# Handing some bf16-bit shifts of an attention kernel from VectorE to GpSimd

## The chip, the cores and the metric

The kernel runs on one core of a Trainium2 chip. The metric is the device time of one execution, in microseconds. Before the change it is 1596.61 us, the median of three runs (1596.51 to 1596.66).

## The reference

The reference is a stack of four residual layers on x of 2048 tokens by 512 channels: attention, MLP, attention, MLP, all in bf16, each after a layer norm. Both attentions use the same weights, and so do both MLPs.

```python
def _A_ref(x, wqkv, wo):            # 32 heads of 16 channels
    q, k, v = ...                   # from x @ wqkv
    scores = jnp.einsum("bhqd,bhkd->bhqk", q, k) * Dh ** -0.5
    p = _softmax(scores, axis=-1)
    o = jnp.einsum("bhqk,bhkd->bhqd", p, v)
    return o.transpose(0, 2, 1, 3).reshape(B, S, D) @ wo

def _B_ref(x, w1, b1, w2, b2):
    h = _gelu(jnp.einsum("bsd,df->bsf", _layernorm(x), w1) + b1)
    return jnp.einsum("bsf,fd->bsd", h, w2) + b2

x = x + _A_ref(_layernorm(x), A_wqkv, A_wo)
x = x + _B_ref(_layernorm(x), B_w1, B_b1, B_w2, B_b2)
# and both once more
```

What matters here is the softmax: 32 heads x 2048 x 2048 exponentials in each attention.

## The kernel before

**The work.** The layers are called L = 1 and L = 3 (each with the MLP behind it). The queries are cut into units of 512 tokens, qc (in L = 3 the last unit is cut into two of 256). The heads are in eight groups of four, hg. A *segment* is one head group of one unit against all 2048 keys (the first unit of each layer is cut into two parts by keys). It consists of score tiles: one key block of 128 tokens, one head, 512 query columns; a full segment has 16 x 4 = 64 of them. For each tile PE multiplies keys and queries into a PSUM bank (L1401, four heads side by side in rows of the array), something turns scores into exponentials, and PE multiplies those with the values into bank ACCB (L1579, four heads side by side in columns). The 17th column of the values is ones, so that the softmax's denominator comes along.

**Two ways to an exponential.** ScalarE takes two or three tiles at once from PSUM and writes bf16 into PT (L1386). In five of sixteen key blocks (DK = 3, 6, 9, 12, 15) a tile may go to VectorE instead, which uses the fact that a number written as an integer into the bits of a bf16 is roughly its exponential. The *load* (`d_load`, L1478) adds BITS0 to the scores in PSUM and writes them as uint16 into a slot of `dp`; read as bf16, this is a rough exponential. To make it exact enough, three more *readings* of it are made, with 32, 64 and 96 added to the bits (SHIFT; `job_d`, L1509), each into a `dp` slot of its own, and PE sums all four with values that are scaled by WSHIFT (`vs`, L1169, made by GpSimd and kept in DRAM). Two tiles make a batch (DBATCH), so that a reading is one instruction of 1024 elements.

**What sets the order.** Nothing is written by hand. A planner on the host (`Sched`, `Prog`) simulates the engines with a cost for each operation, and the order in which it picks tasks becomes the fixed order of each engine's instructions; semaphores for the dependencies are added at the end. It picks, for each engine, the ready task of least priority number (`best`), and then the engine whose pick comes first (`run`). What it takes for true of costs is in `Prog.op` (L106): VectorE is free again 0.08 us before an operation's end (OVERLAP). An operation marked "fast" on VectorE becomes longer by the last GpSimd operation's `hit` where the two overlap (L140 to L147):

```python
if eng == "pool":
    self.hit = (op.t0, op.t0 + dur, lat or 0.0)
elif lat == "fast":
    if self.hit[0] < op.t0 + dur and op.t0 < self.hit[1]:
        dur += self.hit[2]
```

**How many tiles VectorE gets** is decided while planning. `take_d` (L1411) hands it a tile if VectorE isn't booked over 1.3 us ahead and has no more than DBACK = 2.0 us of tasks pending, if a slot of `dp` is free and fewer than DFLY = 4 batches are under way, and if a PSUM bank is free: DLANE (bank 5), or MISCB (bank 7). It is called beside every group for ScalarE (`flow_scores`), after every VectorE operation (`d_solo`), and in gaps of PE (`fill_pe`). Tiles that nobody took by the segment's end go to ScalarE. So VectorE's planned free time turns into tiles that ScalarE needn't do. `refill` then puts matmuls of zeros (L1307, L1309, L1311) into gaps of PE.

**Around the change.** `job_d` is started when a batch's loads are in the plan. For each of the three readings it gets a `dp` slot, sets a priority and submits the task. It goes on to the next when the task has been planned (not when it has ended). The priority `pr` is 0.15 if no tile of the segment is left and it is the one being summed, 0.5 if fewer than DURGE = 8 are left, and 2.5 else: behind all else that VectorE has. `try_pv` (L1526) plans the value matmuls of a reading when its planned end is at most PV_NEAR = 0.7 us away; PE's order is then fixed. GpSimd's other work is Q scaling (`job_qt`, L1144), the scaled values (L1169), layer norm (L858 to L868), and the small operations of the score bound and of the joining of the two parts (L1003 to L1007, L1622 to L1633).

Of the kernel before, what the change touches and what calls it, by code (L numbers as in the profile page):

```python
# [14 lines left out]
ALU = mybir.AluOpType  # L15
# [20 lines left out]
SHIFT = (0, 32, 64, 96)  # L36
# [231 lines left out]
def I(fn, reads=(), writes=(), dur=0.3, same_ok=(), lat=None):  # L268
    return (fn, tuple(reads), tuple(writes), tuple(same_ok), dur, lat)
# [242 lines left out]
class Builder:  # L512
# [988 lines left out]
    def job_d(self, bt):  # L1501

        S_ = self.S_
        u, n, sg = bt["unit"], len(bt["tiles"]), bt["tiles"][0][0]
        N = 512 * n
        for k in range(1, len(SHIFT)):
            v = yield ("get", "dp", sg["i"])
            pr = 0.15 if not self.left(sg) and sg is self.segs[self.acc_seg] else 0.5 if self.left(sg) < DURGE else 2.5
            yield Task("dve", pr, [I(lambda e, k=k, v=v: e.tensor_scalar(out=self.dp[:, v, 0:N], in0=self.dp[:, u, 0:N], scalar1=float(SHIFT[k]), scalar2=None, op0=ALU.add),  # L1509
                                     [("dp", u, w) for w in range(n)], [("dp", v, w) for w in range(n)] + self.dres(v), 0.150 + 0.2605e-3 * N, (), "fast")])  # L1510
            self.d_ready(bt, k, v, range(n))
        self.flying -= 1
        self.use_done(("dp", u))
# [425 lines left out]
```

## Time and profile before

| engine | part of the work | instructions | busy us | mean ns |
|---|---|---|---|---|
| PE | scores, L1401 | 4608 | 672.3 | 358 |
| PE | value matmuls of PT, L1579 | 3544 | 467.1 | 358 |
| PE | value matmuls of the load and the three readings, L1579 | 4256 | 659.7 | 357 |
| ScalarE | exponentials, L1386 | 1274 | 1449.7 | 1259 |
| VectorE | loads, L1478 | 944 | 632.6 | 681 |
| VectorE | readings, L1509 | 1434 | 557.4 | 430 |
| GpSimd | Q scaling, L1144 | 84 | 72.2 | 860 |
| GpSimd | scaled values, L1169 | 72 | 60.5 | 842 |

The profiled execution has a span of 1594.1 us, with TensorE's clock fully granted. Durations overlap: VectorE starts the next instruction before the last has ended, and four matmuls run side by side on PE, so that a group's busy time isn't instructions times mean. A busy digit is the share of a fortieth of the span (40 us) in tenths:

```profile
DVE  7689999989999899989999898999899989999793
ACT  6999999999999999989999998999999999999996
POOL 5585312001220012103212217310001000020010
```

GpSimd is busy at the start (layer norm and the bounds of the first layer) and around 1000 us, and nearly idle else. The waits of VectorE and ScalarE, longest first, are these:

```profile
DVE dp L1478 <- PE ps L1401: 58.2, 81, 3.0
DVE xres L1758 <- PE ps L1756: 15.5, 8, 4.2
...
ACT PT L1386 <- PE ps L1401: 32.2, 80, 4.4
ACT h L1810 <- PE ps L1713: 11.8, 4, 8.1
```

The numbers are the sum in us, the times, and the longest.

### The profile page before, as it was taken

The page shows a single profiled execution, that of the slowest core. Times are in us where ns is not written, and L with a number is a line of the kernel's source. Part 1 is how long each engine was busy: PE and PEld are TensorE (multiplying, and loading weights), DVE is VectorE, ACT ScalarE, POOL GpSimd, SP SyncE. Part 2 cuts the span into 40 slices and gives each one's busy share as a digit, 9 for nine tenths or more (in the row PEclk, how much of TensorE's full clock was granted, in tenths as well). Part 3 has the DMA queues.
Part 4 walks back from the last instruction along what each step waited for, and adds up shares of the span by engine and source line. Part 5 has one row for each costly group of instructions (what it writes and reads, how often), then busy time and mean ns, then how long its engine had stood idle before and what let it go on. Part 6 is the DMA issues. An engine that isn't in the chain of part 4 may idle for free.

```text
span 1594.1 us, 39159 instructions
## 1 busy us (share of the span) xinstructions
PE 1538.6 (97%) x16364; PEld 479.4 (30%) x16497; DVE 1450.3 (91%) x3202; ACT 1528.0 (96%) x1357; POOL 333.9 (21%) x574
## 2 busy tenths in 40 slices
PE   9999999999999999999999999999999999999998
PEld 3222222222222222222222223222222222344444
DVE  7689999989999899989999898999899989999793
ACT  6999999999999999989999998999999999999996
POOL 5585312001220012103212217310001000020010
PEclk9999999999999999999999999999999999999999
DMA  6662012112321223223722233211101100221100
GB/s 172 116 142 87 29 31 40 48 41 59 81 48 50 44 53 78 57 53 86 139 44 62 53 68 78 61 25 21 34 14 38 28 19 22 40 48 30 41 25 21
DMA packets 212465, 88.80 MB, mean 56 GB/s; under 512 B 183835, under 2 KB 206656, under 8 KB 212288
## 3 DMA queue, kind: packets, MB, share of 16 engines
q1 hardware_dynamic: 212288, 86.29, 24.0%
q8 instruction: 129, 2.11, 0.6%
q14 instruction: 48, 0.39, 0.1%
HBM read 34.65 MB, written 19.48 MB: 34 GB/s over the span
## 4 chain that ended last, share of the span: by engine, by line
PE 51%; DVE 28%; ACT 17%; issue 2%; POOL 0%; DMA 0%; POOLq 0%; DVEq 0%
PE ps L1401 18%; ACT PT L1386 15%; PE ps L1579 15%; DVE dp L1478 12%; DVE dp L1509 9%; PE ps L1713 4%; PE ps L1756 4%; PE ps L927 3%; PE ps L1307 3%; ACT h L1748 1%; PE ps L1311 1%; PE ps L1658 1%; DVE accT L1609 1%; DVE st L850 1%; DVE n L992 1%
## 5 line engine op out<-in xcount | busy, mean ns | idle before, releaser
L1386 ACT ACTIVATE PT<-ps 128x1536 bf16<-128x1536 f32 (+1 forms) x1274 | 1449.7, 1259 | 38.8 <-PE ps L1401 32.2
L1401 PE MATMUL ps<-QT,KT 32*128 32x512 bf16 (+1 forms) x4608 | 672.3, 358 | 16.8 <-DVE dp L1478 5.5
L1478 DVE TENSOR_SCALAR dp<-ps 128x512 uint16<-128x512 f32 x944 | 632.6, 681 | 61.2 <-PE ps L1401 58.2
L1509 DVE TENSOR_SCALAR dp<-dp 128x1024 uint16<-128x1024 uint16 (+1 forms) x1434 | 557.4, 430 | 7.9 <-PE ps L1579 3.2
L1579 PE MATMUL ps<-PT,V 128*17 128x512 bf16 (+1 forms) x3544 | 467.1, 358 | 0.0
L1579 PE MATMUL ps<-dp,vs 128*17 128x512 bf16 (+1 forms) x3192 | 444.4, 357 | 0.5 <-DVE dp L1509 0.2
L1401 PEld LDWEIGHTS ps<-QT,KT 32*128 32x128 bf16 x4608 | 172.2, 91 | 546.4 <-ACT PT L1386 237.3
L1144 POOL TENSOR_SCALAR QT<-qraw,scl,qbias 128x512 bf16<-128x512 bf16 (+1 forms) x84 | 72.2, 860 | 790.0 <-PE ps L1401 784.8
L1579 PE MATMUL ps<-dp,V 128*17 128x512 bf16 (+1 forms) x1064 | 215.3, 357 | 1.3 <-DVE accT L1609 1.0
L1309 PE MATMUL ps<-zw 32*128 32x444 bf16 (+5 forms) x702 | 193.5, 323 | 0.0
L1579 PEld LDWEIGHTS ps<-dp,vs 128*17 128x17 bf16 x3192 | 111.0, 88 | 130.3 <-issue 106.8
L1579 PEld LDWEIGHTS ps<-PT,V 128*17 128x17 bf16 x3544 | 113.2, 88 | 102.5 <-issue 89.6
L1311 PE MATMUL ps<-zw 128*32 128x448 bf16 (+22 forms) x1477 | 136.5, 323 | 0.4 <-DVE dp L1478 0.2
L1307 PE MATMUL ps<-zw 128*128 128x448 bf16 (+17 forms) x481 | 114.1, 333 | 4.0 <-DVE ps L727 1.7
L1713 PE MATMUL ps<-yT,wf 128*128 128x512 bf16 (+3 forms) x353 | 92.9, 356 | 8.6 <-issue 4.4
L927 PE MATMUL ps<-wqkv,xnT 128*128 128x512 bf16 x299 | 85.8, 382 | 7.6 <-issue 3.5
L1609 DVE STREAM_TRANSPOSE accT<-ps 128x512 f32<-128x512 f32 (+1 forms) x88 | 57.9, 658 | 10.8 <-PE ps L1579 9.9
L1737 DVE TENSOR_SCALAR h<-ps,b1c 128x512 bf16<-128x512 f32 (+2 forms) x88 | 62.3, 708 | 5.0 <-PE ps L1713 4.7
L1579 PEld LDWEIGHTS ps<-dp,V 128*17 128x17 bf16 x1064 | 53.1, 88 | 45.2 <-issue 27.3
L1169 POOL TENSOR_SCALAR vs<-V 128x340 bf16<-128x340 bf16 (+2 forms) x72 | 60.5, 842 | 26.3 <-PE ps L1579 21.2
L1307 PEld LDWEIGHTS ps<-zw 128*128 128x128 bf16 x481 | 37.4, 98 | 74.2 <-issue 46.4
L1311 PEld LDWEIGHTS ps<-zw 128*32 128x32 bf16 x1477 | 49.1, 95 | 22.1 <-DVE dp L1478 4.1
(179 smaller groups left out, 892.2 us busy)
## 6 DMA issues: line engine op xcount, KB each, us to landing
vs<-vs_scr SPq DMA_DIRECT2D x56, 255.0 KB, 2.8
wf<-in_B_w_dram SPq DMA_DIRECT2D x90, 128.0 KB, 2.6
q_scr<-qk SPq DMA_DIRECT2D x22, 256.0 KB, 2.1
k_scr<-qk SPq DMA_DIRECT2D x12, 256.0 KB, 2.0
out_dram<-xres SPq DMA_DIRECT2D x16, 128.0 KB, 1.7
vs_scr<-vs SPq DMA_DIRECT2D x8, 255.0 KB, 2.9
xres<-in_A_x_dram SPq DMA_DIRECT2D x7, 256.0 KB, 3.3
v_scr<-vst SPq DMA_DIRECT2D x12, 136.0 KB, 1.7
```

The costliest lines, as they stand in the source:

```text
L927: yield Task("pe", prio, [I(lambda e, c=c: e.matmul(self.ps[:, b, :], lhsT=xnT[:, c, :], rhs=self.wqkv[:, c, which * 512:which * 512 + 512 ...
L1144: yield Task(eng, 0.4, [I(lambda e: e.tensor_scalar(out=self.QT[:, q, 0:W], in0=src, scalar1=self.scl[:, k, hg:hg + 1], scalar2=self.qbias ...
L1307: fn = lambda e: e.matmul(self.ps[:, b, 0:w], lhsT=self.zw[:, 0:128], rhs=self.zw[:, 0:w], start=st, stop=st, skip_group_check=True)
L1309: fn = lambda e: e.matmul(self.ps[:, b, 0:w], lhsT=self.zw[32 * p:32 * p + 32, 0:128], rhs=self.zw[32 * p:32 * p + 32, 0:w], start=st, sto ...
L1311: fn = lambda e: e.matmul(self.ps[32 * p:32 * p + 32, b, 0:w], lhsT=self.zw[:, 0:32], rhs=self.zw[:, 0:w], start=st, stop=st, skip_group_c ...
L1386: S_.submit(Task("act", 1e-5 * gi, [I(lambda e, pt=pt, n=n, b0=b0: e.activation(out=self.PT[:, pt:pt + n, :], in_=self.ps[:, b0:b0 + n, :] ...
L1401: return [I(lambda e, kb=kb, i=i: e.matmul(self.ps[:, b, i * W:(i + 1) * W], lhsT=self.KT[32 * hp:32 * hp + 32, hg, kb * 128:(kb + 1) * 12 ...
L1478: self.S_.submit(Task("dve", 0.0, [I(lambda e: e.tensor_scalar(out=self.dp[:, u, w * 512:(w + 1) * 512], in0=self.ps[:, b, :], scalar1=BIT ...
L1509: yield Task("dve", pr, [I(lambda e, k=k, v=v: e.tensor_scalar(out=self.dp[:, v, 0:N], in0=self.dp[:, u, 0:N], scalar1=float(SHIFT[k]), sc ...
L1579: ops.append((nth[j, sh] + 0.1 * i, I(lambda e, hp=hp, v=v, ap=ap[:, i * W:(i + 1) * W], first=first and i == 0, W=W: e.matmul(self.ps[32 ...
L1609: yield Task("dve", 0.3, [I(lambda e: e.transpose(self.accT[:, a, 0:W], self.ps[:, ACCB, 0:W]), [("ps", ACCB)], [RA], 0.17 + 0.535 * W / 5 ...
L1713: yield Task("pe", pr, [I(lambda e, c=c: e.matmul(self.ps[0:M, b, off:off + W], lhsT=self.w1(fc, c), rhs=self.yT[:, c, 0:W], start=(c == 0 ...
```

## The change

A reading may now be planned for GpSimd. That is so if it is not urgent (`pr > 1.0`, that is 2.5), if GpSimd in the plan is free within 0.3 us, and if none of its pending tasks is ready within 0.5 us. `k in (1, 2, 3)` is true of all three readings. Else the reading goes to VectorE as before. The planner takes a GpSimd reading to last 0.25 + 1.3e-3 x 1024 = 1.58 us (on VectorE 0.150 + 0.2605e-3 x 1024 = 0.417 us), and a "fast" VectorE operation that overlaps it to last 0.09 us longer. What is computed stays the same. The aim is to take work from VectorE, which is nearly full, to an engine that is nearly empty.

```diff
         for k in range(1, len(SHIFT)):
             v = yield ("get", "dp", sg["i"])
             pr = 0.15 if ... else 0.5 if self.left(sg) < DURGE else 2.5
-            yield Task("dve", pr, [I(lambda e, k=k, v=v: e.tensor_scalar(out=self.dp[:, v, 0:N], in0=self.dp[:, u, 0:N], scalar1=float(SHIFT[k]), scalar2=None, op0=ALU.add),
-                                     [...], [...], 0.150 + 0.2605e-3 * N, (), "fast")])
+            eng = "pool" if k in (1, 2, 3) and pr > 1.0 and S_.P.free["pool"] <= S_.now + 0.3 and not any(S_.task_ready(t) <= S_.now + 0.5 for t in S_.pend["pool"]) else "dve"
+            yield Task(eng, pr, [I(lambda e, k=k, v=v: e.tensor_scalar(out=self.dp[:, v, 0:N], in0=self.dp[:, u, 0:N], scalar1=float(SHIFT[k]), scalar2=None, op0=ALU.add),
+                                     [...], [...], 0.150 + 0.2605e-3 * N if eng == "dve" else 0.25 + 1.3e-3 * N, (), "fast" if eng == "dve" else 0.09)])
             self.d_ready(bt, k, v, range(n))
```

More of the change, by code (lines that the diff above doesn't have):

```diff
@@ L1508, in job_d @@
             pr = 0.15 if not self.left(sg) and sg is self.segs[self.acc_seg] else 0.5 if self.left(sg) < DURGE else 2.5
-            yield Task("dve", pr, [I(lambda e, k=k, v=v: e.tensor_scalar(out=self.dp[:, v, 0:N], in0=self.dp[:, u, 0:N], scalar1=float(SHIFT[k]), scalar2=None, op0=ALU.add),
-                                     [("dp", u, w) for w in range(n)], [("dp", v, w) for w in range(n)] + self.dres(v), 0.150 + 0.2605e-3 * N, (), "fast")])
+            eng = "pool" if k in (1, 2, 3) and pr > 1.0 and S_.P.free["pool"] <= S_.now + 0.3 and not any(S_.task_ready(t) <= S_.now + 0.5 for t in S_.pend["pool"]) else "dve"
+            yield Task(eng, pr, [I(lambda e, k=k, v=v: e.tensor_scalar(out=self.dp[:, v, 0:N], in0=self.dp[:, u, 0:N], scalar1=float(SHIFT[k]), scalar2=None, op0=ALU.add),
+                                     [("dp", u, w) for w in range(n)], [("dp", v, w) for w in range(n)] + self.dres(v), 0.150 + 0.2605e-3 * N if eng == "dve" else 0.25 + 1.3e-3 * N, (), "fast" if eng == "dve" else 0.09)])
             self.d_ready(bt, k, v, range(n))
```

## The prediction

> **What bounds the kernel now.** I read the page's busy shares first, then the chain, the table of stretches, the groups split by shape, the waits of ScalarE and VectorE, and last the timeline around single GpSimd instructions.
>
> ```profile
> PE 1538.6 (97%) x16364; PEld 479.4 (30%) x16497; DVE 1450.3 (91%) x3202; ACT 1528.0 (96%) x1357; POOL 333.9 (21%) x574
> PE 51%; DVE 28%; ACT 17%; issue 2%; POOL 0%; DMA 0%; POOLq 0%; DVEq 0%
> ```
>
> PE's 97% is no bound: the zero-weight fillers (L1307, L1309, L1311) stand at 114, 194 and 137 us in the page's groups, and the planner drops them where real matmuls need the room. The chain hops between scores (L1401), exponentials (L1386) and the Schraudolph loads and readings (L1478, L1509). The table of stretches tells more:
>
> ```profile
> 100.00:400.00 300.00, 289.21 (x2926) 81.82 (x2951) 281.03 (x622) 294.79 (x263) 79.72 (x140) 1.00 0.22 54
> 400.00:700.00 300.00, 291.63 (x2728) 78.71 (x2754) 283.34 (x614) 294.18 (x251) 46.06 (x76) 1.00 0.23 56
> 700.00:1000.00 300.00, 289.37 (x2859) 85.30 (x2880) 279.72 (x615) 283.72 (x249) 90.69 (x156) 1.00 0.35 75
> 1000.00:1300.00 300.00, 292.77 (x2998) 81.79 (x3013) 285.10 (x623) 296.86 (x260) 32.15 (x48) 1.00 0.15 30
> ```
>
> The columns after the length are PE, weight loads, VectorE, ScalarE, GpSimd. In these 1200 us ScalarE is busy 1169.6 us (97.5%) and VectorE 1129.2 us (94.1%). The work is a balance of two full engines: a score tile is either an exponential on ScalarE or a load and three readings on VectorE. GpSimd is nearly empty (248.6 of 1200 us).
>
> ```profile
> L1386 ACT ACTIVATE PT<-ps 128x1536 bf16<-128x1536 f32 x605 | 897.1, 1483 | 21.0 <-PE ps L1401 14.9
> L1386 ACT ACTIVATE PT<-ps 128x1024 bf16<-128x1024 f32 x668 | 700.8, 1057 | 17.8 <-PE ps L1401 17.4
> L1478 DVE TENSOR_SCALAR dp<-ps 128x512 uint16<-128x512 f32 x944 | 632.6, 681 | 61.2 <-PE ps L1401 58.2
> L1509 DVE TENSOR_SCALAR dp<-dp 128x1024 uint16<-128x1024 uint16 x1398 | 548.9, 433 | 7.6 <-PE ps L1579 2.9
> L1144 POOL TENSOR_SCALAR QT<-qraw,scl,qbias 128x512 bf16<-128x512 bf16 x68 | 62.1, 914 | 601.9 <-PE ps L1401 596.8 <-DVE scl L1113 5.1
> ```
>
> A tile of 512 columns more or less on ScalarE is 1483 - 1057 = 426 ns. ScalarE waited only 39 us before all exponentials, so today's stalls hardly reach it.
>
> The timeline shows how GpSimd and VectorE meet. At 250 us, VectorE then GpSimd:
>
> ```profile
> 250.53 1.09 DVE L1509 TENSOR_SCALAR dp<-dp 128x1024 uint16<-128x1024 uint16 x3
> 251.54 0.68 DVE L1682 TENSOR_TENSOR xres<-ps,xres 128x512 bf16<-128x512 f32 x1
> 250.54 1.56 POOL L1144 TENSOR_SCALAR QT<-qraw,scl,qbias 128x512 bf16<-128x512 bf16 x1 [13.30 <-PE ps L1401]
> ```
>
> and at 784 us, in the same order:
>
> ```profile
> 784.15 0.69 DVE L1478 TENSOR_SCALAR dp<-ps 128x512 uint16<-128x512 f32 x1
> 784.76 0.81 DVE L1509 TENSOR_SCALAR dp<-dp 128x1024 uint16<-128x1024 uint16 x1
> 784.52 0.77 POOL L1144 TENSOR_SCALAR QT<-qraw,scl,qbias 128x512 bf16<-128x512 bf16 x1 [6.93 <-PE ps L1401]
> ```
>
> In the first the readings came first and GpSimd stood until all three were through: 1.56 us for what takes 0.77 us alone. In the second GpSimd was 0.24 us into its instruction when the reading came, and the reading took 0.81 us in place of 0.42 us. The load from PSUM beside it (0.69 us) was not touched. A run of three readings takes 1.09 us, so a reading occupies VectorE (1.09 - 0.42) / 2 = 0.335 us; a load occupies 250.53 - 249.94 = 0.59 us.
>
> [...]
>
> **The change, part by part.** *How many move.* 1434 readings are 478 batches of three, one batch each 3.1 us between 93 and 1562 us. A reading is not urgent while 8 or more of its segment's tiles (mostly 64) are left, 56/64 = 87%. GpSimd is idle about 80% of the time. The first reading of a batch thus goes to GpSimd in 0.87 x 0.8 = 70% of the batches, 335 readings. The second then finds GpSimd busy for over 0.3 us; a third reaches it again if VectorE let the second lie. An upper end is one reading per planned 1.58 us of the idle 1140 us between 100 and 1500 us, 720. I take 430, range 300 to 650.
>
> *What leaves VectorE.* 430 x 0.335 = 144 us.
>
> *What GpSimd pays.* No 1024-element uint16 reading on it is in the trace. From below: L1144 takes 0.55 us at its shortest (256 elements) and 0.77 at its median (512), so 0.43 us for each 512 more, and 1.2 us for 1024. [...] From above: L1169 grows from 0.72 us at 204 to 1.06 at 340 elements, 2.5 ns an element, so 2.8 us, but in rows of 68. I take 1.3 us alone and 1.7 with waits; the planner has 1.58. 430 x 1.7 = 730 us on an idle engine cost nothing in themselves.
>
> *What the lock gives back.* For 512 elements the delayed readings of both L1144 and L868 end near 1.05 us after GpSimd's start, 0.42 after 0.63; a reading that came 0.12 us after GpSimd's start passed, one at 0.17 us was held. The lock is some 0.46 us. The mean 1024-element reading is 433 ns and the median 419: 1398 x 14 ns = 20 us of waits, over 194 long GpSimd instructions (68 + 54 + 72), 0.1 us each. For 1024 elements the lock is 0.46 + 0.42 = 0.9 us[...]. Both the chance of a hit and the length of the wait grow with it, so 0.1 x (0.9 / 0.46) squared = 0.38 us; readings come in bursts, and GpSimd begins behind one, beside the loads, which makes it less. I take 0.3 us, range 0.15 to 0.6. So the chip gives back 430 x 0.3 = 129 of the 144 us.
>
> *What the planner believes.* It charges a VectorE reading 0.09 us when it overlaps GpSimd's last instruction; one or two do, 0.13 us. It sees 430 x (0.335 - 0.13) = 88 us free and takes more tiles for VectorE, each 0.59 + 1.5 x 0.335 = 1.1 us, less what moves, about 1.0. As ScalarE shortens by 0.43 us a tile, x tiles balance where 1.0 x = 88 - 0.4 x: x = 63. Planned gain: 63 x 0.43 = 27 us. PE takes 189 more value matmuls (L1579) in place of fillers, at nothing.
>
> *On the chip.* The order is fixed when it is written. VectorE gets 430 x (0.3 - 0.13) = 73 us more than planned, with some 83 us of idle time (5.9% of 1400 us) spread in pieces. I let 60% pass through, 44 us. The added wait is in PE's queue: value matmuls wait for GpSimd's reading, and the scores behind them, which ScalarE waits for, stand too. PE has slack against ScalarE (its weight loads wait 237 us for L1386 in all, 0.39 us a time), so I add only 3 us. Sum: 1597 - 27 + 44 + 3 = 1617. The tests that pick the engine cost the chip nothing; GpSimd's own queue (Q scaling, layer norms) is one reading later at most, with no one waiting (0.3 us behind L1144 in all).
>
> **The rivals.** *The lock costs what is charged, 0.13 us:* GpSimd runs mostly beside PSUM loads. For it: the loads don't contend and two follow in each batch. Against it: VectorE is 94% full and a reading comes about each microsecond. Then the planned gain stands: 1597 - 27 = 1570. *GpSimd is slow:* at 2.5 ns an element it takes 2.8 us, PE waits over 1 us for each, and VectorE's wait exceeds the 0.335 saved by far; with 300 moved and about 0.8 us each, half passing through, 1597 + 120 = 1717. Against it: the contiguous instructions grow at 0.8 ns. *Few move, or the plan takes no more tiles:* the tiles of five in sixteen key blocks qualify and 944 are used, so there is room, but PSUM banks and reading buffers may hold it: about 1597.
>
> **How the numbers follow.** Lock gives the saving back, 1617: 0.52. Planned gain stands, about 1570: 0.33. Slow GpSimd, about 1717: 0.08. No difference: 0.07. Faster by over 0.2% 0.33, same 0.07, slower 0.60. Wait ends: 0.15 us gives 1597 - 27 + 5 = 1575; 0.6 us gives 430 x 0.47 x 0.6 = 121, so 1691. The range from 1568 to 1682 takes in the faster rival and most of the wait's bounds, and leaves out the slow GpSimd.
>
> **What would show it.** GpSimd's busy time should rise by 500 to 1000 us, with a new group dp<-dp of 300 to 650, 1.3 to 2.0 us each. The median of VectorE's readings should stay at 419 ns while the mean goes from 433 to 500 or more. The L1478 loads should grow from 944 to about 1007, and the exponentials shrink by 27 us. ScalarE's wait before L1386 should grow from 39 us to some 80. I am wrong if that wait stays under 50 us (then faster), if GpSimd's group is above 2.3 us, or if the loads stay near 944.

## The result and the profile after

The kernel takes 1879.3 us (median of four runs, 1877.05 to 1882.93) where it took 1596.6 us: a ratio of 1.177, with a 95% interval of 1.175 to 1.180. The forecast of 1617 us had the direction and missed the size: 283 us were lost, not 20.

The busy shares and the chain on the page of the kernel after:

```profile
PE 1687.5 (90%) x16161; PEld 484.0 (26%) x16161; DVE 1600.8 (85%) x2880; ACT 1548.6 (83%) x1348; POOL 1421.9 (76%) x956
PE 36%; DVE 35%; POOL 22%; issue 5%; ACT 1%; DMA 0%; SPq 0%; POOLq 0%; DVEq 0%
```

ScalarE, busy for 96% of the time before, is at 83%, and the chain has 22% of GpSimd in it where it had none. VectorE, from which work was taken, is busy for 151 us more. The groups split by shape (busy us, mean ns of one, idle time before, and who ended it):

```profile
L1510 POOL TENSOR_SCALAR dp<-dp 128x1024 uint16<-128x1024 uint16 x382 | 1104.8, 2901 | 346.4 <-DVE dp L1478 282.5 <-PE ps L1580 24.9 <-DVE dp L1510 14.4
L1386 ACT ACTIVATE PT<-ps 128x1536 bf16<-128x1536 f32 x601 | 875.3, 1456 | 220.5 <-PE ps L1401 215.7
L1510 DVE TENSOR_SCALAR dp<-dp 128x1024 uint16<-128x1024 uint16 x1040 | 646.6, 653 | 27.5 <-PE ps L1580 10.4 <-POOL dp L1510 8.9 <-issue 3.1
L1478 DVE TENSOR_SCALAR dp<-ps 128x512 uint16<-128x512 f32 x965 | 643.4, 679 | 148.8 <-PE ps L1401 135.5 <-POOL dp L1510 7.5 <-PE ps L1714 1.6
```

Three things stand here. 382 readings moved, and each takes 2.9 us on GpSimd, where the planner counted on 1.58. The 1024-element readings that stayed on VectorE take 653 ns each where they took 433. And only 21 more loads were planned (965 against 944). The waits say who pays:

```profile
ACT PT L1386 <- PE ps L1401: 288.9, 335, 9.4
PEld ps L1580 <- POOL dp L1510: 112.2, 102, 3.6
PE ps L1580 <- POOL dp L1510: 75.4, 72, 3.1
```

ScalarE waits 288.9 us for scores (32.2 before), 257 us more, about the whole loss of 283 us. The last two rows are PE's weight loads and its matmuls, and they overlap in time: together PE stands 112 us before value matmuls whose reading GpSimd hasn't ended (none before; the expectations below add the two rows to 188). The timeline from 512 us shows how PE's wait becomes ScalarE's; GpSimd, PE and ScalarE in turn:

```profile
512.41 5.50 POOL L1510 TENSOR_SCALAR dp<-dp 128x1024 uint16<-128x1024 uint16 x2
517.97 0.38 PE L1580 MATMUL ps<-dp,vs 128*17 128x512 bf16 x1 [2.13 <-POOL dp L1510]
519.40 1.45 ACT L1386 ACTIVATE PT<-ps 128x1536 bf16<-128x1536 f32 x1 [2.59 <-PE ps L1401]
```

GpSimd makes two readings in 5.5 us (3.2 in the plan). PE has come to a value matmul of the second and stands 2.13 us, with the next scores behind it in the order. When they come, ScalarE has stood 2.59 us.

VectorE's readings tell when GpSimd's hold them up. This table is counted from the change's trace: all 1024-element readings of VectorE by the time at which they start after the start of GpSimd's reading.

```text
start after GpSimd's, us   readings   median ns
0.0 to 0.2                  45        1225
0.2 to 0.4                 116        1257
0.4 to 0.6                  36         880
0.6 to 0.8                  13         653
0.8 to 1.0                  19         652
1.0 to 1.2                  22         416
1.2 to 1.4                  69         414
1.4 to 1.6                  51         414
1.6 to 1.8                  35         414
1.8 to 2.0                  58        1207
2.0 to 2.2                  32        1200
2.2 to 2.4                  28         804
2.4 to 2.6                  25         610
```

During one of GpSimd's readings VectorE's are held up twice (two *spells*), with a gap from about 1.0 to 1.7 us in which they take their usual 0.41 us. A reading that comes early in a spell takes some 0.84 us longer (1257 - 419 ns). The prediction's *lock* and the *port* of the theories and forecasts below are names for this. The runs show for how long a reading is held up, not by what.

### The profile page after: what moved, and what is told of

Read it like the earlier page. It is cut to its first block, busy times and chain, and to the rows that moved or that the text cites. A ratio compares the mean times of both kernels' runs of the same rounds, so it can differ in the third digit from the quotient of the medians.

```text
span 1875.4 us, 38860 instructions
## 1 busy us (share of the span) xinstructions
PE 1687.5 (90%) x16161; PEld 484.0 (26%) x16161; DVE 1600.8 (85%) x2880; ACT 1548.6 (83%) x1348; POOL 1421.9 (76%) x956
## 4 chain that ended last, share of the span: by engine, by line
PE 36%; DVE 35%; POOL 22%; issue 5%; ACT 1%; DMA 0%; SPq 0%; POOLq 0%; DVEq 0%
POOL dp L1510 17%; DVE dp L1478 14%; DVE dp L1510 13%; PE ps L1401 12%; PE ps L1580 11%; PE ps L1757 3%; PE ps L927 2%; PE ps L1714 2%; PE ps L1307 2%; POOL QT L1144 1%; DVE h L1738 1%; DVE accT L1610 1%; POOL vs L1169 1%; ACT PT L1386 1%; POOL xn L868 1%
## 5 line engine op out<-in xcount | busy, mean ns | idle before, releaser
L1386 ACT ACTIVATE PT<-ps 128x1536 bf16<-128x1536 f32 (+1 forms) x1265 | 1469.2, 1233 | 295.8 <-PE ps L1401 288.9
L1510 POOL TENSOR_SCALAR dp<-dp 128x1024 uint16<-128x1024 uint16 x382 | 1104.8, 2901 | 346.4 <-DVE dp L1478 282.5
L1401 PE MATMUL ps<-QT,KT 32*128 32x512 bf16 (+1 forms) x4608 | 712.5, 375 | 59.2 <-DVE dp L1478 51.7
L1510 DVE TENSOR_SCALAR dp<-dp 128x1024 uint16<-128x1024 uint16 (+1 forms) x1091 | 663.4, 640 | 28.1 <-PE ps L1580 10.4
L1580 PE MATMUL ps<-dp,vs 128*17 128x512 bf16 (+1 forms) x3267 | 497.9, 378 | 93.7 <-POOL dp L1510 75.4
L1580 PE MATMUL ps<-PT,V 128*17 128x512 bf16 (+1 forms) x3519 | 495.8, 372 | 0.7 <-ACT PT L1386 0.5
L1309 PE MATMUL ps<-zw 32*128 32x444 bf16 (+3 forms) x691 | 204.1, 342 | 0.3 <-DVE accT L1610 0.3
L1311 PE MATMUL ps<-zw 128*32 128x448 bf16 (+23 forms) x1116 | 121.4, 337 | 4.1 <-DVE dp L1478 3.7
L1307 PE MATMUL ps<-zw 128*128 128x448 bf16 (+20 forms) x442 | 111.9, 349 | 4.8 <-DVE dp L1478 2.8
L1144 POOL TENSOR_SCALAR QT<-qraw,scl,qbias 128x512 bf16<-128x512 bf16 (+1 forms) x84 | 70.6, 841 | 3.9 <-PE ps L1401 2.7
L1169 POOL TENSOR_SCALAR vs<-V 128x340 bf16<-128x340 bf16 (+2 forms) x72 | 60.8, 846 | 7.7 <-PE ps L1580 3.5
L1309 PEld LDWEIGHTS ps<-zw 32*128 32x128 bf16 x691 | 54.9, 94 | 4.1 <-issue 1.5
```

The costliest lines, as they stand in the source:

```text
L1144: yield Task(eng, 0.4, [I(lambda e: e.tensor_scalar(out=self.QT[:, q, 0:W], in0=src, scalar1=self.scl[:, k, hg:hg + 1], scalar2=self.qbias ...
L1307: fn = lambda e: e.matmul(self.ps[:, b, 0:w], lhsT=self.zw[:, 0:128], rhs=self.zw[:, 0:w], start=st, stop=st, skip_group_check=True)
L1309: fn = lambda e: e.matmul(self.ps[:, b, 0:w], lhsT=self.zw[32 * p:32 * p + 32, 0:128], rhs=self.zw[32 * p:32 * p + 32, 0:w], start=st, sto ...
L1311: fn = lambda e: e.matmul(self.ps[32 * p:32 * p + 32, b, 0:w], lhsT=self.zw[:, 0:32], rhs=self.zw[:, 0:w], start=st, stop=st, skip_group_c ...
L1386: S_.submit(Task("act", 1e-5 * gi, [I(lambda e, pt=pt, n=n, b0=b0: e.activation(out=self.PT[:, pt:pt + n, :], in_=self.ps[:, b0:b0 + n, :] ...
L1401: return [I(lambda e, kb=kb, i=i: e.matmul(self.ps[:, b, i * W:(i + 1) * W], lhsT=self.KT[32 * hp:32 * hp + 32, hg, kb * 128:(kb + 1) * 12 ...
```

## The experiments

The theories: *lateness* (GpSimd hands a reading over later than planned, PE stands in order, ScalarE runs dry), and *port* (VectorE's readings take longer beside GpSimd's). Ahead of both stands the question why the reading takes 2.9 us at all. "Wait per moved reading" below is the number of VectorE's 1024-element readings times their mean over 419 ns (the median before), less the 20 us of the kernel before, by the number of GpSimd's readings. For the change it is (1040 x 0.234 - 20) / 382 = 0.58 us. A time given without a ratio is that of a single execution. A *plan's end* is the time at which the planner on the host lets the last operation end: 1587.5 us for the kernel before, 1573.9 us for the change.

### What a reading costs on GpSimd

```diff
+ # behind the end, three times each: dp <- dp of 1024 (one of 512) on GpSimd
+ tensor_scalar(u16, 32.0, add); the same with 512; tensor_scalar(bf16, 0.5, mult)
+ tensor_scalar(u16, 32.0, add, 0.0, add)
+ tensor_scalar(u16, c0, add); tensor_scalar(u16, c0, add, c1, add)   # c0, c1 in SBUF
+ tensor_scalar(bf16, c0, mult, c1, add)
```

> The kernel before, with GpSimd readings of several forms behind its end, three times each, when VectorE does nothing. The rows theory (L1169's 2.5 ns an element comes from its rows of 68): the change's instruction (1024 uint16, one added number) takes about 1.2 to 1.5 us. The form theory (an instruction with one plain number takes 2.5 ns an element, one with two operations whose numbers come from SBUF, as L1144, 0.84): the change's instruction takes 2.76 us (as its shortest in the change's trace), its half of 512 about 1.4 to 1.5 us, the same with bf16 2.76 us, and the form with two operations and numbers from SBUF 1.2 us, also on uint16. The type theory (uint16 is slow): both uint16 forms take 2.76 us and both bf16 forms less.

The run's time, 1653.91 us, includes them. Its timeline on GpSimd, the first row of each form (L1893 to L1899 in the order of the diff):

```profile
1594.44 2.79 POOL L1893 TENSOR_SCALAR dp<-dp 128x1024 uint16<-128x1024 uint16 x1
1597.31 1.49 POOL L1894 TENSOR_SCALAR dp<-dp 128x512 uint16<-128x512 uint16 x1
1598.88 2.79 POOL L1895 TENSOR_SCALAR dp<-dp 128x1024 bf16<-128x1024 bf16 x1
1601.75 3.64 POOL L1896 TENSOR_SCALAR dp<-dp 128x1024 uint16<-128x1024 uint16 x1
1608.44 3.79 POOL L1898 TENSOR_SCALAR dp<-dp,shc 128x1024 uint16<-128x1024 uint16 x1
1612.33 1.19 POOL L1899 TENSOR_SCALAR dp<-dp,shc 128x1024 bf16<-128x1024 bf16 x1
```

The rows theory falls: the change's own instruction takes 2.79 us alone. My form theory had the right rows but the wrong feature: two operations with numbers from SBUF take 3.79 us if both add. The number's place hardly matters (L1897 takes 2.85 us). Quick is a multiply followed by an add: 1.19 us. This is called the quick form below, the single add the slow one. The type was left open here, since the quick one was bf16; the next run shows it.

### The same order, with the quick form (f2)

```diff
- tensor_scalar(dp, dp, SHIFT[k], None, add)                 # on GpSimd only
+ tensor_scalar(dp, dp, 1.0, SHIFT[k], mult, add)            # the same numbers
```

> The change with its order unchanged; only GpSimd's readings are written as times 1.0 plus the shift (the same numbers), a form that took 1.19 us on bf16. If it is as quick on uint16, a reading ends before the planned 1.58 us and holds the port once. The planned gain then stands but for the port: 1597 - 27 + 430 x (wait - 0.13), so 1570 to 1610, PE's waits for GpSimd under 20 us in place of 188, VectorE's mean reading 450 to 500 ns in place of 640. If uint16 is slow in this form too: about 1880.

1668.93 us, ratio 1.046 (1.044 to 1.047). By shape:

```profile
L1518 DVE TENSOR_SCALAR dp<-dp 128x1024 uint16<-128x1024 uint16 x1040 | 586.9, 596 | 8.4 <-PE ps L1585 3.1
L1519 POOL TENSOR_SCALAR dp<-dp 128x1024 uint16<-128x1024 uint16 x382 | 436.5, 1145 | 761.4 <-DVE dp L1478 598.0 <-PE ps L1585 80.8 <-DVE dp L1518 30.5
```

The multiply-add is quick on uint16 too: 1.04 us at its shortest, 1.15 on average. With not one instruction moved, 210 of the 283 us are back. So most of the loss is the price of the plain add. But 72 us are left, with GpSimd now earlier than planned. VectorE's readings stand at 596 ns: (1040 x 0.177 - 20) / 382 = 0.43 us of wait for each moved reading, which had taken 0.335 us on VectorE. The move costs VectorE more than it takes from it. There is one spell: in f2's trace readings that start 1.0 us or later after GpSimd's start have medians of 408 to 417 ns. I had expected 450 to 500 ns and at most 1610 us.

The waits show how this reaches ScalarE:

```profile
PEld ps L1401 <- DVE dp L1478: 167.1, 341, 1.5
ACT PT L1386 <- PE ps L1401: 94.6, 199, 2.7
```

The loads come later behind the held readings, so the PSUM banks that they read come free later, and PE, in its order, stands before the next scores: 167.1 us in this row, 66.7 before. ScalarE then waits 62 us more for scores than before, most of the 72. VectorE has 56% of the chain, 28% before.

### The slow form, with the planner told its length

```diff
- ... else 0.25 + 1.3e-3 * N
+ ... else 0.25 + 2.65e-3 * N
```

> The change with the planner told 0.25 + 2.65e-3 x 1024 = 2.96 us for GpSimd's reading (slow form; 300 readings move, 949 loads). Lateness theory (PE stands in order before values that GpSimd hands over 1.3 us later than planned): 1580 to 1620, PE's waits for GpSimd under 30 us. Port theory (VectorE's readings, held by GpSimd, set the time): 300/382 of the loss stays, 1780 to 1850, and VectorE's mean reading stays at 600 ns or more.

1732.56 us. PE's waits for GpSimd are gone, all but one row of the waits:

```profile
PEld ps L1580 <- POOL dp L1510: 2.8, 6, 1.1
```

Yet 136 us stay, of which 17 are in the plan already (it ends at 1604.3 us). VectorE's readings have a mean of 618 ns, 0.66 us of wait for each of 300 moved. Pure lateness would have given 1580 to 1620: it isn't the whole cause. The port theory, at 1780 or more, is too high as well.

### The port alone

```diff
  # the kernel before; in job_d, where the change would hand a reading to GpSimd:
+ submit GpSimd: tensor_scalar(dum, wo[0:640], 32.0, None, add)    # nobody reads dum
```

> The kernel before with 390 GpSimd readings in the slow form beside it, 640 elements each, into a tile that nobody reads (the planner knows their 1.83 us, 935 loads, all readings on VectorE). Nobody can be late. Lateness theory: 1600 to 1620. Port theory: VectorE waits for the port for 390 x 0.63 of the change's blocking, so 1720 to 1780.

1744.5 us: work that nobody waits for, on an engine that was idle, costs 148 us (8 of them in the plan, which ends at 1595.5 us), as the port theory had it. VectorE's readings take 553 ns (1389 x 0.134 - 20 = 166 us of waits), and ScalarE waits 153.5 us for scores. The same in the quick form, which had one spell in f2:

> As the kernel with idle readings, in the multiply-add form: 556 readings of 640 elements that nobody waits for (938 loads). If the port is what costs there (1745 with 390 readings of two spells, 148 us, so 0.19 us a spell), 556 single spells give 1596 + 106 = 1700, within 25 us. If GpSimd's length as such costs (1.97 us against about 0.8), 1660 or less.

1720.73 us (the plan's end is that of the kernel before). GpSimd's instructions take 0.82 us on average where they took 1.97, and 556 spells in place of 780 (one and two for each, as in f2 and in the change; an estimate for these 640 elements) cost 124 us in place of 148. This speaks for the spells and against the length, which would have left 64 us or less; a spell costs somewhat more here than there, 0.22 us for 0.19. VectorE's waits are (1386 x 0.121 - 20) = 148 us. In both runs the loss is close to these waits.

### Lateness alone

```diff
  # the order of the change, the quick form, and ahead of each reading on GpSimd:
+ tensor_tensor(shc[8 numbers], half, half, pow)             # 1.77 us
```

> The order of the change; GpSimd's readings in the multiply-add form, each behind a power of eight numbers a partition (about 1.7 us, hardly a use of the port), so that it ends as late as in the change, 2.9 us, but holds the port for one pass. Lateness theory: 1830 to 1900, PE's waits for GpSimd near 188 us. Port theory: 1600 to 1680.

1780.48 us, between the ranges of the two theories. Against the same order without the power (1669), a reading that ends 1.7 us later costs 112 us, while the power holds up no reading of VectorE (those that start beside it have medians of 412 to 420 ns). PE's waits for GpSimd are back, 114 us (the two rows overlap). VectorE's readings wait less, 511 ns: shifted by 1.7 us, GpSimd meets them less often, and their waits come to 75 us in place of 164. So the 112 us are no upper bound of what lateness costs.

### Can the port be planned around?

If the planner knew when GpSimd holds readings up, it could put loads there:

```diff
+ def port(self, t): return self.lock[1] if self.lock[0] - 0.3 <= t < self.lock[1] else t
  # a "fast" operation on VectorE starts at port(t0); GpSimd's starts behind the last fast one
- 0.25 + 1.3e-3 * N ... 0.09
+ 0.23 + 0.85e-3 * N ... 0.85e-3 * N       # the multiply-add form; the last is how long the planner lets it hold readings up
```

> The multiply-add form, and a planner that knows the port: a reading on VectorE that would start while GpSimd's reading holds it (0.87 us, from 0.12 us after its start) is not ready until then, so that loads go first, and GpSimd's waits for a reading that VectorE is at. 546 readings move, 952 loads. If the port explains what is left of the loss in f2 (1669), the chip follows this plan: 1585 to 1615, VectorE's mean reading under 480 ns. If something else does (PSUM banks, the reading buffers held longer, GpSimd's late ends), it stays near 1650.

1625.23 us, ratio 1.019 (1.018 to 1.020), between the two; VectorE's mean reading is 552 ns, not under 480. It is 44 us better than f2's order with 546 readings moved in place of 382.

```profile
PE 1549.5 (95%) x16224; PEld 477.1 (29%) x16363; DVE 1409.8 (87%) x2679; ACT 1529.6 (94%) x1354; POOL 910.0 (56%) x1120
L1490 DVE TENSOR_SCALAR dp<-ps 128x512 uint16<-128x512 f32 x952 | 635.8, 681 | 118.7 <-PE ps L1413 110.5
L1530 DVE TENSOR_SCALAR dp<-dp 128x1024 uint16<-128x1024 uint16 x861 | 450.1, 552 | 10.7 <-PE ps L1597 8.9
```

(The lines are shifted by 12 to 20: L1490 is the load, L1530 the reading.) The wait per moved reading falls from 0.43 to (861 x 0.133 - 20) / 546 = 0.17 us, and VectorE is less busy than before the change (1409.8 us against 1450.3). Still the kernel is 29 us slower: the loads wait 110.5 us for scores (58.2 before), and ScalarE 58.3 us (32.2). Little was to be had in any case, as this plan ends at 1586.0 us, 1.5 us before that of the kernel before. Why a VectorE with room doesn't help is not settled by a run. What is known is that the number of loads hardly grows with it, 952. Counting in `take_d` why it refuses VectorE a tile (some 2300 times) gives this for the kernels before and after:

```text
                          before   after
no PSUM bank              1630     1782
no slot of dp              336      376
two loads pending          134      149
four batches under way      83       31
VectorE's tasks > 2.0 us    80       48
```

In `take_d` VectorE's tasks were the reason in 80 cases before, PSUM banks in 1630. But the table is not the whole account. `d_solo`, which asks `take_d` after each operation of VectorE, first holds back when VectorE is booked for over 1.2 us, with the tasks that are soon ready: in 2300 of 4141 calls before and 1764 of 3840 after. And in 1060 of the 1630 cases the bank DLANE was held by a tile whose load was not planned yet. So VectorE's own time kept tiles from it often, and whether it or the banks limit the loads stays open; more banks were not tried, since the kernel's `ps` has eight and all are in use.

### Only the third reading

In f2 GpSimd's reading often starts beside a sibling of the same batch on VectorE. If the siblings make the hits, the last of the three should be free of them:

```diff
- eng = "pool" if k in (1, 2, 3) and pr > 1.0 and ...
+ eng = "pool" if k == 3 and pr > 1.0 and ...            # multiply-add, 0.23 + 0.85e-3 * N
```

> The multiply-add form, and only the third reading of a batch may go to GpSimd (k == 3; planner told 0.23 + 0.85e-3 x 1024 = 1.10 us; 271 move, 963 loads). In f2 382 moved, 255 of them held a VectorE reading by 0.64 us on average, mostly a sibling of the same batch that was ready at the same moment. Sibling theory: without siblings under a third of the 271 hold one, VectorE's mean reading is under 470 ns, and the time is 1580 to 1600. Chance theory (any reading of the next microsecond is hit): half or more hold one, mean 520 ns or more, 1615 to 1645.

1676.07 us, ratio 1.049 (1.046 to 1.053), with 271 readings moved:

```profile
L1518 DVE TENSOR_SCALAR dp<-dp 128x1024 uint16<-128x1024 uint16 x1151 | 603.5, 559 | 13.4 <-PE ps L1585 5.0 <-POOL dp L1519 2.9
```

Fewer moves, and a larger wait for each: (1151 x 0.140 - 20) / 271 = 0.52 us. The time is above the ranges of both theories. The sibling theory's forecast fails, but the run does not test it: `job_d` goes on to the third reading when the second has been planned, not when it has ended, so that the second can still be ahead of VectorE when GpSimd starts. With the batches followed through the planner's order, 212 of the 271 have a held reading of VectorE (over 500 ns) start inside GpSimd's span; with 151 of them it is a sibling, mostly the second reading, and with 61 one of another batch. Both happen, and siblings more often.

### The form, where it costs nothing

```diff
  # the kernel before, L1169, on GpSimd
- scalar1=WSHIFT[k], scalar2=None, op0=ALU.mult
+ scalar1=WSHIFT[k], scalar2=0.0, op0=ALU.mult, op1=ALU.add
```

> The kernel before with its order unchanged and all readings on VectorE; only GpSimd's 72 scaled-value instructions (L1169) are written as a multiply and an add of 0.0. The form theory: 0.45 to 0.65 us for 340 elements in place of 1.06, one spell on the port in place of two. As they lie on an idle engine, the gain is what VectorE waits for them at most: 0 to 4 us.

1592.32 us, ratio 0.9977 (0.9969 to 0.9986): a little faster than the kernel before, and the only one here that is. The first line is of the kernel before, the others of this run:

```profile
L1169 POOL TENSOR_SCALAR vs<-V 128x340 bf16<-128x340 bf16 x24 | 26.6, 1109 | 6.1 <-PE ps L1579 4.8
L1169 POOL TENSOR_SCALAR vs<-V 128x340 bf16<-128x340 bf16 x24 | 11.9, 496 | 6.1 <-PE ps L1579 4.8
L1509 DVE TENSOR_SCALAR dp<-dp 128x1024 uint16<-128x1024 uint16 x1398 | 542.3, 428 | 7.9 <-PE ps L1579 3.3
```

The 340-element instruction falls from 1109 to 496 ns, and VectorE's mean reading from 433 to 428 ns, 1398 x 5 ns = 7 us. Not all of this is less waiting for GpSimd, since the median falls too, from 419 to 417 ns. That the 4 us gained come from there is likely, but not shown apart.

## Why the prediction was wrong

**The price of the reading: wrong, and the largest error.** The step "I take 1.3 us alone and 1.7 with waits" chose L1144's rate of 0.84 ns an element and put L1169's 2.5 ns down to its rows of 68. The rows cost nothing: in the quick form 340 elements in such rows take 474 ns at their shortest, and the 0.72 and 1.04 us of 640 and 1024 contiguous elements put 340 at 0.47. What differs is that L1144 multiplies and then adds. The change's instruction is of L1169's kind, 2.79 us alone and 2.90 in place. With the quick form and nothing else changed, 210 of the 283 us are back. The prediction's own sign of being wrong, a GpSimd group above 2.3 us, has come true. The range of the cost held the value, at its upper end; the rival built on it, 0.08, was the right mechanism, though it too fell short (1717).

**What waits for GpSimd: wrong.** "I add only 3 us" let PE's slack against ScalarE hide a late reading. With the price right that might have held: in f2 PE's waits for GpSimd are too short to be listed. At 2.9 us it did not: 112 us of PE waits, and 112 us of time for lateness alone. What the step didn't have is PE's wait for VectorE's loads, which a held reading delays: in f2 its row grows by 100 us.

**What the lock gives back: right in kind, low.** I worked out 0.38 us for one spell of 0.9 us and took 0.3; f2 measures 0.43 for that form. The spell itself was right: in f2 a reading that starts 0.07 us after GpSimd's takes 1269 ns, so it is held until about 0.9 us after GpSimd's start. For the form of the change it is 0.58 us, in two spells with a gap from about 1.0 to 1.7 us, which the prediction didn't have. That PSUM loads aren't touched holds: 679 ns with GpSimd busy for 76% of the time, 681 before. In the change's trace the 564 of 965 loads that start inside a GpSimd reading take 679 ns, and so do the other 401.

**How many move: right.** 382, of the 430 forecast.

**What the planner believes: wrong by three in tiles, by two in time.** The step turned 88 us of freed VectorE time into 63 tiles and 27 us. The plan took 21, and ends 14 us earlier. Why so few is open: the step let VectorE's time alone decide, and the counts show that PSUM banks and `dp` slots refuse tiles too, without saying which of them limits.

**How much passes to the end: too little.** I let 60% of the unplanned VectorE time through. With VectorE's readings held up and nothing late, 140 us (148 less the 8 in the plan) of 166 us of waits passed in one run (e3) and 124 of 148 in the other (e4), some 84%. VectorE's idle time, spread in pieces, absorbed some 16%.

Put together: in f2's order the loss is 72 us. Lateness adds 112 us to it, or more, since the waits of VectorE's readings fell in that run, from 164 to 75 us. What is left of the change's 283 us, 99 us or less, I put down to the second spell and to how both act together; no run shows these apart.

A part of this is TensorE's clock. The share that was granted, in tenths, of the kernel before and after:

```profile
PEclk9999999999999999999999999999999999999999
PEclk9999987978999899999999999989998998899989
```

It was 0.94 on average in the change (1.00 before). The trace has 29 stretches of 3.4 to 20.5 us, 222 us in all, with the clock granted at half; the kernel before has none until its last matmul. A score matmul takes 566 ns there and 358 elsewhere. In the 4 us ahead of a stretch PE stood for 49% of the time (24 to 74%), in other 4 us for 9%. By the scores done, 104 of the 281 us by which the profiled span grew fall into these stretches; at the rate of loss in the rest of the run it would be 24 us, so the halved clock costs some 80 us, an estimate that takes the waits to cost no more there than elsewhere. It came with lateness: f2's order has one such stretch of 3.4 us (clock 0.999), the same order with late readings has 20, of 137 us (0.962), and 74 of the 185 us lost there fall into them. So much of what lateness costs may come by way of the clock. No run kept the clock up with readings late, so the share is not shown by experiment.

## What to carry to other kernels

Price a moved operation by a row of the same form on the new engine, with the same operations in the instruction, not by one of the same shape; if the trace has rows of two prices, the form has to be settled before the cheaper one is taken. Work on an idle engine isn't free if it makes the instructions of a full one longer: 390 instructions whose results nobody used cost 148 us here. Where PE is made to stand, look at its granted clock (0.94 here, 1.00 before) before the loss is put down to the waits alone. And before freed time is turned into a gain, ask what else limits the work that should fill it.

## What the runs showed of the hardware

On GpSimd a `tensor_scalar` with a multiply and an add took 1.04 us at its shortest for 1024 uint16 (f2), and 1.19 us for bf16 with numbers from SBUF (m1). One add of uint16 or one multiply of bf16 took 2.79 us, and two adds 3.64 us (m1). So an add took less than half the time with a multiply by one ahead of it (2.90 us in the change, 1.15 in f2), and so did a multiply with an add of zero behind it (1109 ns before, 496 in h1, for 340 bf16); an add of zero behind an add made it slower (2.79 and 3.64 us). VectorE's 1024-element readings, 419 ns in the median of the kernel before, took up to 1257 ns in the median beside GpSimd's slow form, in two spells, until about 1.0 us and again from 1.8 to 2.7 us after its start (the change). Beside the quick one there was one spell, until about 1.0 us (f2). In the change TensorE's granted clock fell to half in 29 stretches of 3.41 to 20.48 us, each behind 4 us in which PE had stood for 24 to 74% of the time.
